# An RWKV attention and channel-mixing kernel: twenty-two transposes taken from TensorE to VectorE and DMA, a new order of the work, hidden values at another address

## The chip, the cores and the metric

The kernel runs on one core of one Trainium2 chip, as one program. The metric is the device time of one execution in microseconds; lower is better. Engines are called as in the profile: PE (TensorE, matrix products; PEld is its weight load), DVE (VectorE), ACT (ScalarE), POOL (GpSimd), SP (the queue that issues all DMAs of this kernel).

## What is computed

Four batches, eight heads, 768 time steps, head dimension 48; then a mixing of the 768 steps with a rank of 32, and a feed-forward part with 384 -> 1536 -> 384 channels. All in float32.

```python
state = 0                                        # per batch and head, 48 x 48
for t in range(768):
    cur = outer(u * k[t], v[t])
    y[t] = r[t] @ (state + cur)
    state = w[t][:, None] * state + outer(k[t], v[t])
x  = y as [batch, 768, 384]
h  = (x.transpose(0, 2, 1) @ U) @ V              # U: 768 x 32, V: 32 x 768
u_ = x + h.transpose(0, 2, 1)
out = u_ + relu(u_ @ w_ch1) @ w_ch2              # 384 x 1536, 1536 x 384
```

## The kernel before, in words

**Tiling.** The 768 steps of a batch are cut into 6 chunks of 128, so there are 24 chunks, numbered 0 to 23 over the batches; heads are handled in four pairs. For each chunk DMAs load the decays (LW), r and k with channels on the partitions (LRK), r and k with time on the partitions (LKR) and v (LV). DVE runs scans of the decays (F, Q), POOL or DVE scale r and k by them (RP, KS). PE then makes the scores inside the chunk (AM), a DVE copy under a mask merges them (CP), and PE forms the chunk's part of y from them (YA) and from the state carried in (YZ). The state is carried on by DS: per head the product of k and v, summed over the 128 steps. For DS, k is needed with time on the partitions, and the scaled k has channels there. So PE turns it (KT: four transposes of 128x128 into PSUM) and ACT or DVE copies the result to SBUF (KN, tile kn).

**x.** The finished y of a chunk is copied to SBUF with channels on the partitions (XE, tile xT). The mixing over time contracts over time, so x is turned as well: XT is three transposes of 128x128 on PE, XN the copy to SBUF (tile xn). Then come the sums with U: for batch 0 a chain GW of six steps, one per chunk, which adds into one PSUM tile; for the other batches GA in two parts (chunks 0 to 3, each in its own quarter of the array's columns, then 4 and 5), a copy G4 and one product SELM that adds the four quarters. The result is split into a high and a low part (GS, GSL), and HP multiplies it by V for each of three channel tiles. u_ is formed and split into high and low parts (UADD, UH, UL).

**Feed-forward.** float32 products are made from three products of a reduced type: high x high, low x high, high x low. For each half batch of 384 steps there are twelve UP steps (one per 128 hidden channels) and twelve DN steps (three channel tiles, four parts each). Every UP and every DN is a group of nine matmuls of 128x384; the text calls it a group. Behind each UP, ACT or DVE write the high part (HH) and DVE the low part (HL) of the hidden values, tiles hh and hl, taken from PSUM tiles of which three exist. They lie in a pool of 24 equal buffers. Small uint8 tiles named gap... shift the addresses of what follows them.

**Order.** Each of these is a step with an engine, the steps it comes after, and the buffers it takes and gives back. A string ORDER of three characters a step (number, and how) fixes the order in which all steps are written, the engine where there is a choice (`alt`), and how many units of idle matmuls (`warm`) PE does first. Each engine runs its instructions strictly in that order. SP is one such queue: a DMA that waits for a buffer holds back every DMA behind it. Weights are loaded as bits and split in the first part of the run (LRAW, AB, E, C1, C2, SG, ADD, HI, SUB).

In lines: KT and KN are `turn_k` (L532) and `copy_k`; XT and XN are in `turn` (L668 and `back`); GA, G4, SELM and GW are in `token_mix` (L691, L697, L701, L720); UP is L824, HL L837, DN L859, the last sum O L874 and its store OUT L878. The address of a buffer follows from the sizes ahead of it in its pool: in this kernel the u tiles start at 201792 (64 modulo 256 bytes) and the first of the hidden buffers at 100032 (192 modulo 256), all others of a pool being whole multiples of 256 bytes further.

Of the kernel before, what the change touches and what calls it, by code (L numbers as in the profile page):

```python
# [8 lines left out]
F32 = mybir.dt.float32  # L9
# [6 lines left out]
AF = mybir.ActivationFunctionType  # L16
# [6 lines left out]
P = 128  # L23
# [16 lines left out]
HALF = P // 2  # L40

# [5 lines left out]
def channel_order():  # L47
# [13 lines left out]
    "3i03j03k03n03v03o13p03q03w+3r13s03x04804B03y14904a03m00704J04D03+O4E03-04d04b01b01104004A03z14K6500090080420"  # L61
    "4e15104L04G04100c04F14QG0K04C14f04M14l14N14m00A04g04i00B05S01204R04400001c00C11J01e04h11401305T00D04c04n04sC"
    "4314q01d03l05301504o01f04r05B14p01610E00H05805501g14O04P04t05600F05CM4500e01715415u05711804V05V08e01910104W0"
    "0I01L05D04S00301h05205E00L04X05X04T05d15a05Y05F05G05I01i01j05H05v04Y00T04x04U14y05x05J04Z00M08U04z04605y15Z1"
    "4700200d04u04v00400f04w10N05z00g05e05f05K05k00O08v06315i05g05U00512900P15h05j05+05W15N00600h15L05M11t06409M0"
    "0G08u08X06505-10i15O06F05P00l06605l04+06001K08V06G05p00J00j00k15m05w06718f14-05Q01u01M00Q00V01v01w09U00R00S0"
    "1N01O16801x05q08g15n05R06906H01A08x01P15r05s05o15t06A48c06B00U08Z01y19006C00n08z08a08b11z06I06J08h06D08W0920"
    "9108i08j06N08y16E08+09K01C08k00W01Q00X08l06K01S08o01+01R16L00Y18-08m06M08n08d09m09L00Z09801B01-06O06P06S06T0"
    "0m01D06U00a12B01E06Q06V06X06Y06Z09A09V08Y16a00b06W08q06f02A02C09301F19416R02D01U0DA01G11k09n02E19509N00o06b0"
    "6c09601H02F02R06g02G00p07709901I19P00q12H06d06h07109Q09W07808w09701T06e06x01m07901V01l00r01W07201n00u01X06y0"  # L70
    "1o06i07301p16z01Y19S10s08p06u01Z08r02j01q19X06j06v01a12009B09a01r00t01s09b06+00v08s09p02k09R12S06k00w02l09F0"
    "0x00y09G0Af09c02U09C00z12m0Ao08t09u12V00+16w07S07T0A009r02T02W19O12I09Y02n09Z00-09s0A102o16r06s16t06-01009D0"
    "2102X17402s09E17507009d02209H02302406l02p02q19t12512612a02Y02r16m02-07606o02J06n02K02L02713Q06p02M02802N12O1"
    "A209h09i09e03807W06q09I02Z17X07a07U07b02b02c02d02P02e07A09j07B02t02f02Q12u07C02g03002v02h02w03102i17D09v03Z0"
    "7G03903202x02y13H0Ae03A03303B07Y09T03403513C02z07V12+13D17E03603J07H07I07c13I03717F03E03F07Z1AC03a03K09w03G0"
    "3L07d17J03M1AF03R03b03N17K03c09J13S03O03P17M07n08309q07o0An09x19f0AE08407N03T0AH08503d03e1AD03f19k07k0AK13U0"
    "3V13W17p07l18003X07m07e03g18109g1Ap19o0Aq0820AG17h09l0Ah0Ar0AM07f13Y0AL0AS0Aj0Ak07L0AT13h07i07O07P09y07g07j0"
    "7q0AN1AI07z07Q0Ai1Am09z07r1D90AO07s0860870DZ07R0DJ09+07w0Al1AJ07+08808908A09-0AP0AQ0A30AU0AR0DK1DL0A40A70AV0"
    "E907-0A508B0A61A80Au0A91AW07x0AZ07y0DC0EA1Db0Aa0AA0DM0DI0DH0Dj0As1At1EB0AX07t07u0AB07v0Av0DN0DE0Di0EC0Ag0DF0"
    "D-0Dc0Da0Dk1De0Df0FT0Ab1DO08C08D08E08F0Dg1AY08G08I0DD0E20E30Dl1Aw0FU1Ax0A-0ER0Ac0Ad1E408J08K0Dh0Ay08L0FV1E00"  # L80
    "E71EU08M0Az08N08O0A+0E50E80B00B10Dd0Ea0DP0DG08P0DB0DQ1Dm0EW0Dp0B20Dq1DT0Eb0ED1ES0DU0B30E61DR0B40EF0EE0B50B90"
    "B60EG08Q0Et0DS0Ec1BA0FW08R0BD0B71BB1F10EH0BC0BE0DV0BF08H0EI0B80Dt0BG18S0EZ0Dr0C70BZ0C80Dn1Bi0Ba18T0E10Bj0DW1"
# [12 lines left out]
    "JR0HL0Jm0Jn1Jr0K50JU0J40HV0JS1K00H40J50JV0Jv0Jw0Jx0H51H60H30KE0Js0JW0JX1Jt0KF0HA0HG0HH0Ju0HW1KG0HB1HC0HI0KH0"
    "Jy0HY0HX0KI0Jz1KJ0HZ0KK1IC0ID0HS0HT1HU0Ha0Hb0Hc0Hd0KL0KM0He0KN0Hf0KO0Hg0KP0KQ0KR0KS0KV0K70Hh0Hi03t0KW0Hk05A0"
    "4j0KZ0Hl0KT0KX0KY1Hm0Ka0KU1Kb1Kc1L80Hj0Ky0L91LA0Hn0Kz0K+04k05b0Kv0Kd0Kw1Ke0Ho0Hp0Kf0Kx0Kj05c0Km0Kn1Ko0Kg0610"
    "Kp0Kk1Kl0Kq1Kh0Ki0L50L60K-0L70LB0Kr0L00L10Ks0L20Kt1Ku0LC0LD0L31L40LE0LH0LF0LT0LX0LY0LU0LV1LZ1LI0LJ0La0Lb0LK0"
    "Lc0LG0Ld16204H0Le0LL0LN0LM0LW1LO03u0Lo0LP0M404I0LQ0Lp1Lq0M50LR0M60LS0Lx0Ly1Lz0L+0Ll0Li0Lm1Ln0Lj0Lf0Lk0L-0M00"
    "Lr0Lg0Lh0Lu0Lv1M70Ls0Lt0MA0Lw0M10MB0M80MC0MD0M21M30ME0M90MF0MG0MJ0MK0ML0MM0MH0MN0MO0MP0MQ0MI0MR0MS0MT0MU0"  # L100
# [53 lines left out]
def rwkv_moe_kernel(ctx, tc, wT, rkT, vN, rkN, uB, uT, uD, U, V, w1, w2, out):  # L154
# [90 lines left out]
    const.tile([P, 96], mybir.dt.uint8, name="gap2")  # L245
    ready = {}

    stage.tile([P, 96], mybir.dt.uint8, tag="gap", name="gap3", bufs=1)

    def split_raw(key):  # L250
# [18 lines left out]
        def absolute():  # L269
# [10 lines left out]

        nm = f"{kind}{i}"
# [3 lines left out]
            "E " + nm, "ACT", lambda: nc.scalar.activation(d["w"], d["low"], AF.Copy, scale=2.0**-29), [l], use=[braw],  # L285
# [81 lines left out]
    sts = {}  # L367

    def chunk(g):
# [164 lines left out]
        def copy_k(eng):  # L534
            st["kn"] = sb2.tile([P, NP, P], F32, tag="kn", name=f"kn_{g}")
            copy(eng, st["kn"], st["trk"])
# [123 lines left out]
    def turn(b, c, after, bx, bxn):  # L660
        blk, cc = divmod(c, TB // P)
        btr = Buf("tr")
        d = {}

        def go():
            tr = d["tr"] = psT.tile([P, NP, P], F32, tag="tr", name=f"trx_{b}_{c}")
            for ct in range(NCT):
                nc.tensor.transpose(tr[:, ct, :], blocks[b, blk][:, ct, cc * P : (cc + 1) * P], ident)  # L668

        def back(eng):  # L670
            xn = d["xn"] = sb2.tile([P, NCT, P], F32, tag="xn", name=f"xn_{b}_{c}", bufs=NCH)
# [10 lines left out]
    def token_mix(b):  # L682
# [3 lines left out]
        def part(cs):  # L686
            if cs[0] == 0:
                d["ga"] = psF.tile([P, DM], F32, tag="ffn", name=f"ga_{b}")
            for c in cs:
                p0 = 32 * (c % 4)  # L690
                nc.tensor.matmul(  # L691
                    d["ga"][p0 : p0 + 32, :], U_sb[:, c, :], xns[b, c]["xn"], start=(c < 4), stop=(c >= NCH - 4)
                )
# [5 lines left out]
        def total():  # L699
            d["gb"] = psF.tile([P, DM], F32, tag="ffn", name=f"gb_{b}")  # L700
            nc.tensor.matmul(d["gb"][0 : 3 * RANK, :], sel, d["g4"], start=True, stop=True)  # L701
# [10 lines left out]
        if b == 0:  # L712
            sums, ga = [], None

            def whole(c):
                if c == 0:
                    d["gb"] = psF.tile([P, DM], F32, tag="ffn", name=f"gb_{b}")
                for i in range(3):
                    to = d["gb"][RANK * i : RANK * (i + 1), :]
                    nc.tensor.matmul(to, U_sb[:, c, :], xns[b, c]["xn"], start=(c == 0), stop=(c == NCH - 1))  # L720

            for c in range(NCH):
                ga = step(
                    f"GW {b}.{c}", "PE", lambda c=c: whole(c), xns[b, c]["steps"] + ready.get(("U", 0), []) + [ga],
                    take=[bgb] if c == 0 else [], use=[bgb, xns[b, c]["buf"]],
# [84 lines left out]
    def ffn(b, blk, dst=None):  # L810
# [37 lines left out]
        for ct in range(NCT):  # L848
# [23 lines left out]
            def total(ct=ct):  # L872
                o = blocks[b, blk][:, ct, :]
                nc.vector.tensor_tensor(out=o, in0=d["o", ct], in1=o, op=ALU.add)  # L874

            def send(ct=ct):
                to = out[b] if dst is None else dst
# [212 lines left out]
```

## Time and profile before

| | |
|---|---|
| device time, three runs | 437.16 us median (437.0 to 438.32) |
| the profiled execution | 437.29 us |
| its span, first to last instruction | 435.6 us |
| granted PE clock, mean | 0.997 of full speed (2.4 GHz) |
| busy: PE, PEld, DVE, ACT, POOL | 426.8, 393.8, 285.1, 167.2, 122.9 us |
| all DMA packets, share of 16 DMA engines | 34.6% |

PE is at work all the time that the page can see; the other engines have room, but not everywhere. The page's busy time of a matmul is from its start to its modelled end, and matmuls overlap, so the length of a group is read from the start of its first matmul to the start of the next group's first.

### The profile page before, as it was taken

To read this page: it belongs to the slowest core of one execution; us is meant where nothing else is said; L and a number is where in the kernel's file an instruction comes from. 1 tells how busy PE (TensorE), PEld (TensorE's weight loads), DVE (VectorE), ACT (ScalarE), POOL (GpSimd) and SP (SyncE) were. 2 spreads that over 40 slices of the span, in tenths; PEclk is the share of its full clock that TensorE was granted. 3 is DMA by queue.
4 is the path that set the end of the run, shared out by engine and by line. 5 is a ranking of instruction groups with operands and counts; after the bars stand their busy time and mean duration, and the time that the engine had idled before them with its cause. 6 is when DMAs were issued, how large, how long until landed. Compare 5 with 4: busy or idle time off the path is not lost. (4 is left out here: it accounts for less than half of the span.)

```text
span 435.6 us, 10589 instructions
## 1 busy us (share of the span) xinstructions
PE 426.8 (98%) x4436; PEld 393.8 (90%) x4436; DVE 285.1 (65%) x584; ACT 167.2 (38%) x421; POOL 122.9 (28%) x131
## 2 busy tenths in 40 slices
PE   8989999999999999999999999999999999999995
PEld 4676688999999899999999999999999899999995
DVE  8899999998989778554986259652445145333501
ACT  3989999896251322023332222231231212100200
POOL 6566858433643130210434221111000000010000
PEclk9999999999999999999999999999999999999998
DMA  7988676652526252321532522111000122020001
GB/s 235 372 281 301 190 240 211 202 182 77 157 67 234 84 162 71 93 88 41 167 103 77 167 86 68 58 50 57 20 25 2 42 50 61 0 62 18 2 2 57
DMA packets 21363, 48.58 MB, mean 112 GB/s; under 512 B 2496, under 2 KB 9024, under 8 KB 21312
## 3 DMA queue, kind: packets, MB, share of 16 engines
q1 hardware_dynamic: 21312, 47.87, 34.0%
q8 instruction: 36, 0.59, 0.6%
q14 instruction: 15, 0.12, 0.1%
HBM read 43.14 MB, written 4.72 MB: 110 GB/s over the span
## 5 line engine op out<-in xcount | busy, mean ns | idle before, releaser
L824 PE MATMUL f<-u,w1h 128*128 128x384 f32 x576 | 148.5, 339 | 1.0 <-DVE hl L837 0.7
L824 PEld LDWEIGHTS f<-u,w1h 128*128 128x128 f32 x576 | 102.7, 188 | 2.9 <-DVE hl L837 1.9
L859 PE MATMUL f<-hh,w2h 128*128 128x384 f32 x288 | 98.4, 342 | 0.0
L859 PE MATMUL f<-hl,w2h 128*128 128x384 f32 x288 | 96.9, 336 | 0.0
L859 PE MATMUL f<-hh,w2l 128*128 128x384 f32 x288 | 96.8, 336 | 0.0
L824 PE MATMUL f<-u,w1l 128*128 128x384 f32 x288 | 96.8, 336 | 0.0
L831 ACT ACTIVATE hh<-f 128x384 fp32r<-128x384 f32 x60 | 28.9, 494 | 110.3 <-PE f L824 110.3
L837 DVE SCALAR_TENSOR_TENSOR hl<-f,hh 128x384 fp32r<-128x384 f32 x96 | 51.4, 552 | 27.6 <-ACT hh L831 26.8
L859 PEld LDWEIGHTS f<-hh,w2h 128*128 128x128 f32 x288 | 54.1, 188 | 1.5 <-issue 1.4
L859 PEld LDWEIGHTS f<-hl,w2h 128*128 128x128 f32 x288 | 54.1, 188 | 0.1
L824 PEld LDWEIGHTS f<-u,w1l 128*128 128x128 f32 x288 | 54.1, 188 | 0.0
L859 PEld LDWEIGHTS f<-hh,w2l 128*128 128x128 f32 x288 | 54.0, 188 | 0.0
L783 POOL TENSOR_TENSOR u<-xT,u 128x384 fp32r<-128x384 f32 x10 | 10.6, 1061 | 104.5 <-DVE u L779 97.0
L833 DVE TENSOR_SCALAR hh<-f 128x384 fp32r<-128x384 f32 x36 | 19.8, 552 | 28.9 <-PE f L824 28.8
L874 DVE TENSOR_TENSOR xT<-f,xT 128x384 f32<-128x384 f32 x24 | 13.2, 550 | 31.6 <-PE f L859 25.8
L552 DVE COPY_PREDICATED A<-masks,aps 128x1024 f32<-128x1024 uint32 x24 | 31.7, 1320 | 3.3 <-ACT A L479 2.3
L416 DVE TENSOR_TENSOR_SCAN F<-w,bank 128x129 f32<-128x129 f32 x96 | 32.4, 399 | 1.5 <-issue 1.0
L481 POOL TENSOR_SCALAR_AFFINE_SELECT A<-dv 128x512 f32<-128x512 f32 x31 | 20.6, 677 | 41.7 <-DVE hl L837 17.6
L430 DVE TENSOR_TENSOR_SCAN Q<-w,bank 128x516 f32<-128x516 f32 x24 | 29.3, 1221 | 1.0 <-PE bank L559 0.7
L436 POOL TENSOR_TENSOR rk<-rk,Q 128x512 f32<-128x512 f32 x17 | 20.9, 1228 | 31.9 <-DVE Q L430 18.9
L479 ACT ACTIVATE A<-ident,dv 128x128 f32<-128x128 f32 x68 | 21.3, 390 | 19.0 <-PE trk L532 11.9
L440 POOL TENSOR_TENSOR rk<-rk,F 128x512 f32<-128x512 f32 x17 | 20.8, 1224 | 27.5 <-DVE F L416 22.0
(123 smaller groups left out, 576.8 us busy)
## 6 DMA issues: line engine op xcount, KB each, us to landing
rk<-in_rkT SPq DMA_DIRECT2D x24, 512.0 KB, 4.5
raw_w<-in_w SPq DMA_DIRECT2D x24, 384.0 KB, 4.7
w<-in_wT SPq DMA_DIRECT2D x30, 258.5 KB, 3.0
kr<-in_rkN SPq DMA_DIRECT2D x18, 384.0 KB, 3.9
v<-in_vN SPq DMA_DIRECT2D x24, 224.0 KB, 3.6
out_dram<-xT SPq DMA_DIRECT2D x24, 192.0 KB, 1.9
raw_V<-in_V SPq DMA_DIRECT2D x1, 192.0 KB, 4.0
raw_U<-in_U SPq DMA_DIRECT2D x1, 192.0 KB, 5.7
```

Of the source, the lines that this page charges most:

```text
L416: nc.vector.tensor_tensor_scan(out=out, data0=st["row"][:, j * SEG + 1 : (j + 1) * SEG + 1][:, ::-1], data1=zeros[:, 0:SEG], initial=1.0, ...
L430: nc.vector.tensor_tensor_scan(out=flat(st["Q"]), data0=flat(st["w"]), data1=zeros, initial=1.0, op0=ALU.mult, op1=ALU.add)
L436: ENG[eng].tensor_tensor(out=rk[:, 0], in0=rk[:, 0], in1=st["Q"][:, :, 0:P], op=ALU.mult)
L440: ENG[eng].tensor_tensor(out=k, in0=k, in1=st["F"], op=ALU.mult)
L479: nc.scalar.activation(A[:, i, j], ident, AF.Copy, scale=dv[:, NP * i + j : NP * i + j + 1])
L481: nc.gpsimd.affine_select(out=A[:, i], in_=dv[:, NP * i : NP * i + NP].unsqueeze(2).broadcast_to([P, NP, P]), pattern=[[0, NP], [1, P]], c ...
L552: nc.vector.copy_predicated(by_j(st["A"]), mask8, by_j(st["aps"]))
L824: nc.tensor.matmul(ps, wt[:, f, ct, :], u[ct][:, z], start=(n == 0), stop=(n == 8))
L831: nc.scalar.activation(hh, d["ps", f], AF.Relu)
L833: nc.vector.tensor_scalar(out=hh, in0=d["ps", f], scalar1=0.0, scalar2=None, op0=ALU.max)
L837: nc.vector.scalar_tensor_tensor(out=hl, in0=d["ps", f], scalar=0.0, in1=hh.bitcast(F32), op0=ALU.max, op1=ALU.subtract)
L859: nc.tensor.matmul(d["o", ct], wt[:, 4 * ct + part, f - 3 * part, :], hid[f][z], start=(part == 0 and n == 0), stop=(part == 3 and n == 8),)
```

## The change

Ten of the key turns (chunks 12 to 16 and 18 to 22) and twelve of the x turns (all chunks of batches 2 and 3) no longer go over PE. In their place DVE transposes 32x32 blocks where they stand (KD: one instruction of 128x512; XD: three of 128x128), SP stores the tile to a DRAM buffer (KW, XW), and four DMAs load it back, each into 32 partitions and with the blocks in their new places, in runs of 32 floats (KB, XB). SP issues the four only when the store has landed. The reader (DS or GA) waits for all four.

```diff
+TURN_K = (12,13,14,15,16,18,19,20,21,22)
+TURN_X = (12,13,14,15,16,17,18,19,20,21,22,23)
...
+    def by_dma(kind, nm, after, buf, tile):
...
+            d["at"] = dram.tile(list(t.shape), F32, tag="turn", name=f"turn_{kind}_{nm}", bufs=4)
+            nc.sync.dma_start(d["at"], t)
...
+            t, at = tile(), d["at"].rearrange("(q a) n (s b) -> s a n q b", q=4, s=4)
+            for s in range(4):
+                to = t[32 * s : 32 * s + 32].rearrange("a n (q b) -> a n q b", q=4)
+                nc.sync.dma_start(to, at[s])
...
+        w = step(f"{kind}W {nm}", "SP", there, [after], use=[buf])
+        return step(f"{kind}B {nm}", "SP", back, [w], use=[buf])
...
+            nc.vector.transpose(out=st["kn"].rearrange("p j t -> p (j t)"), in_=st["rk"][:, 1].rearrange("p j t -> p (j t)"))
...
+            if g in TURN_K:
+                kn = step("KD " + nm, "DVE", blocks_of_k, [ks], take=[buf["kn"]], use=[buf["rk"]])
+                kn = by_dma("K", nm, kn, buf["kn"], lambda: st["kn"])
...
+            for ct in range(NCT):
+                nc.vector.transpose(out=d["xn"][:, ct, :], in_=blocks[b, blk][:, ct, cc * P : (cc + 1) * P])
```

The rest: the second part of GA cuts its two matmuls into halves of 192 columns on all four quarters; batch 0 sums its first four chunks by GA and SELM and only the last two by GW; the copy of a turned key leaves out the unused columns; the last sum and its store come in two halves; two of the gap tiles grow by 128 bytes, so that the hidden buffers start at 100160 (64 modulo 256) and u stays at 64; one step of the weights' splitting (E) may run on POOL and does so twice.

```diff
-    const.tile([P, 96], mybir.dt.uint8, name="gap2")
+    const.tile([P, 224], mybir.dt.uint8, name="gap2")
...
+            for n, c in enumerate(cs):
+                for half in range(4 // len(cs)):
+                    p0 = 32 * (n * 4 // len(cs) + half)
...
+            pieces = 2 if (b, blk, ct) == (B - 1, 1, NCT - 1) else 1
```

And the order of all steps is another one; of its table one line of each stands here.

```diff
-    "3i03j03k03n03v03o13p03q03w+3r13s03x04804B03y14904a03m00704J04D03+O4E03-04d04b01b01104004A03z14K6500090080420"
+    "3i03n03j03p03q03o13v13s13k03r13w+3x03+84804B04D04903y10704a03m04b04A01101b03-04J00804E04004G05004d04KM3z1410"
```

Three places show what it does. The first is PE at the end of batch 3's attention, behind YZ of its last chunk, 23 (y_23 is its output, trx the turned x, f1 and f2 the outputs of UP and DN). Before:

```order
L631 MATMUL y_23_4506<-rk_23_3641,Z_22_4476 32x128 x8
L635 MATMUL y_23_4506<-rk_23_3641,Z_22_4476 32x128 x4
L668 MATMUL trx_3_4_4540<-ident_98,xT_3_1_4409 128x128 x3
L859 MATMUL f2_2_1_0_4544<-hh_2_1_0_4173,w2h_127 128x384
L859 MATMUL f2_2_1_0_4544<-hl_2_1_0_4174,w2h_127 128x384
```

Now:

```order
L666 MATMUL y_23_4516<-rk_23_3984,Z_22_4510 32x128 x8
L670 MATMUL y_23_4516<-rk_23_3984,Z_22_4510 32x128 x4
L874 MATMUL f1_2_1_9_4551<-u_2_1_0_3987,w1h_125 128x384 x2
L874 MATMUL f1_2_1_9_4551<-u_2_1_0_3987,w1l_126 128x384
L874 MATMUL f1_2_1_9_4551<-u_2_1_1_4086,w1h_125 128x384 x2
```

The turn of chunk 22's x (3.4) is gone from there, and no other turn follows; ten groups of UP and DN stand between this place and GA, its reader.

The second place is SP for the same x, from the load of v for chunk 23 on (turn_X are the DRAM buffers, 3.3 to 3.5 the chunks of batch 3's second half). Before:

```order
L878 DMA out_dram<-xT_0_2565 128x384
L398 DMA v_4395<-in_vN 128x448
L878 DMA out_dram<-xT_1_3173 128x384
L386 DMA w_0_4671<-in_wT 128x517
L386 DMA w_2_4685<-in_wT 128x517
L878 DMA out_dram<-xT_1_3173 128x384
```

Now:

```order
L424 DMA v_4419<-in_vN 128x448
L384 DMA turn_X_3.4_4549<-xn_4_4496 128x384
L384 DMA turn_X_3.5_4611<-xn_5_4577 128x384
L390 DMA xn_4_4496<-turn_X_3.4_4549 32x12x32 x4
L384 DMA turn_X_3.3_4623<-xn_3_4573 128x384
L390 DMA xn_3_4573<-turn_X_3.3_4623 32x12x32 x4
L390 DMA xn_5_4577<-turn_X_3.5_4611 32x12x32 x4
L932 DMA out_dram<-xT_1_3216 128x384
```

Three stores and twelve loads stand where there was none, and the loads of 3.3 and 3.5 end last.

The third place is SP for the first key that is turned this way, chunk 12. Before, the load of v for chunk 12 and the loads behind it:

```order
L398 DMA v_2360<-in_vN 128x448
L394 DMA kr_2384<-in_rkN 128x768
L390 DMA rk_2391<-in_rkT 128x1024
L381 DMA w_2437<-in_wT 128x517
L394 DMA kr_2459<-in_rkN 128x768
```

Now:

```order
L424 DMA v_2280<-in_vN 128x448
L384 DMA turn_K_2283<-kn_2191 128x512
L390 DMA kn_2191<-turn_K_2283 32x16x32 x4
L407 DMA w_2311<-in_wT 128x517
L416 DMA rk_2359<-in_rkT 128x1024
```

The loads of the decays of chunk 16 and of r and k of chunk 14 now stand behind a wait for a store. DS 12 stands on PE behind the sums of batch 1 (GA, AM 12, SELM), as it did.

## Rows read from the trace of the kernel before

**Rows 1.** The page, part 1: busy us, share of the span, instructions.
```profile
PE 426.8 (98%) x4436; PEld 393.8 (90%) x4436; DVE 285.1 (65%) x584; ACT 167.2 (38%) x421; POOL 122.9 (28%) x131
```

**Rows 2.** Busy time by stretch, in us, with the number of instructions.
```profile
core 0: us, PE busy (x) PEld busy (x) DVE busy (x) ACT busy (x) POOL busy (x), PEclk, DMA share, GB/s
20.00:40.00 20.00, 18.48 (x385) 14.06 (x385) 19.88 (x46) 18.35 (x51) 13.60 (x14) 1.00 0.89 301
67.20:98.50 31.30, 30.62 (x353) 29.23 (x352) 30.59 (x66) 28.66 (x62) 17.50 (x17) 1.00 0.63 199
147.00:200.00 53.00, 53.00 (x574) 50.07 (x574) 34.38 (x69) 14.64 (x39) 11.37 (x11) 1.00 0.35 108
```

**Rows 3.** Groups by line: out<-in, shapes, count | busy us, mean ns | idle before.
```profile
L668 PE MATMUL trx<-ident,xT 128*128 128x128 f32 x72 | 12.5, 282 | 1.0 <-ACT kn L167 0.6 <-ACT xT L167 0.4
L532 PE MATMUL trk<-ident,rk 128*128 128x128 f32 x80 | 12.5, 278 | 0.0
L720 PE MATMUL gb<-xn,U_sb 128*32 128x384 f32 x36 | 4.8, 490 | 0.0
```

**Rows 4.** Timeline of PE around a key turn: start us, length us, what.
```profile
304.12 0.60 PE L532 MATMUL trk<-ident,rk 128*128 128x128 f32 x4
304.48 0.42 PE L859 MATMUL f<-hh,w2h 128*128 128x384 f32 x1
...
306.14 0.51 PE L824 MATMUL f<-u,w1h 128*128 128x384 f32 x2
```

**Rows 5.** Timeline of PE: an HP behind YZ, and an x turn.
```profile
269.79 0.44 PE L765 MATMUL hp<-Vst,gs 96*128 96x384 f32 x1
270.07 0.51 PE L824 MATMUL f<-u,w1h 128*128 128x384 f32 x2
...
276.31 0.49 PE L668 MATMUL trx<-ident,xT 128*128 128x128 f32 x3
276.56 0.59 PE L824 MATMUL f<-u,w1h 128*128 128x384 f32 x2
...
278.20 0.33 PE L765 MATMUL hp<-Vst,gs 96*128 96x384 f32 x1
```

**Rows 6.** Timeline of PE: first and last of eight UP, then of four DN.
```profile
357.85 0.51 PE L824 MATMUL f<-u,w1h 128*128 128x384 f32 x2
...
370.33 0.34 PE L859 MATMUL f<-hh,w2h 128*128 128x384 f32 x1
...
375.03 0.34 PE L859 MATMUL f<-hh,w2h 128*128 128x384 f32 x1
...
381.32 0.51 PE L765 MATMUL hp<-Vst,gs 96*128 96x384 f32 x2
```

**Rows 7.** Timeline of PE: both parts of GA of batch 2.
```profile
238.54 1.46 PE L691 MATMUL ga<-xn,U_sb 128*32 128x384 f32 x12
239.93 0.44 PE L859 MATMUL f<-hh,w2h 128*128 128x384 f32 x1
```

**Rows 8.** Groups by line on DVE, columns as in rows 3.
```profile
L169 DVE COPY kn<-trk 128x512 f32<-128x512 f32 x4 | 2.7, 682 | 1.7 <-PE trk L532 1.7
L169 DVE COPY xn<-trx 128x384 f32<-128x384 f32 x9 | 5.0, 552 | 4.1 <-PE trx L668 4.0
L779 DVE CAST u<-xT 128x384 fp32r<-128x384 f32 x12 | 4.9, 422 | 0.1
```

**Rows 9.** DMA: issues; then packets of 396.7 to 399.2, of 4.2 to 4.95.
```profile
w<-in_wT SPq DMA_DIRECT2D x30, 258.5 KB, 3.0
out_dram<-xT SPq DMA_DIRECT2D x24, 192.0 KB, 1.9
...
q1 hardware_dynamic: 144, 0.20, 22.0%
...
DMA packets 230, 0.22 MB, mean 293 GB/s; under 512 B 160, under 2 KB 160, under 8 KB 230
q1 hardware_dynamic: 230, 0.22, 90.2%
```

**Rows 10.** SP: who waited for whom, us in total, times, longest; an issue.
```profile
SPq L878 <- DVE xT L874: 159.5, 17, 28.2
...
380.53 0.34 SPq L878 DMA_DIRECT2D out_dram<-xT  x1
```

More of the change, by code (lines that the diff above doesn't have):

```diff
@@ L66 @@
[L66 to L70, printed above, removed]
@@ L284, in split_raw @@
         lo = step(
[L285 removed]
+            "E " + nm, "ACT", rounded, [l], use=[braw], alt="Pool",
         )
@@ L688, in part @@
                 d["ga"] = psF.tile([P, DM], F32, tag="ffn", name=f"ga_{b}")
[L689 to L693, printed above, removed]
+            for n, c in enumerate(cs):
+                for half in range(4 // len(cs)):
+                    p0 = 32 * (n * 4 // len(cs) + half)
+                    cols = slice(half * DM * len(cs) // 4, (half + 1) * DM * len(cs) // 4)
+                    nc.tensor.matmul(
+                        d["ga"][p0 : p0 + 32, cols], U_sb[:, c, :], xns[b, c]["xn"].rearrange("p c t -> p (c t)")[:, cols],
+                        start=(c < 4), stop=len(cs) < 4 or b == 0,
+                    )
         def copy4():
@@ L712, in token_mix @@
         if b == 0:
-            sums, ga = [], None
             def whole(c):
-                if c == 0:
-                    d["gb"] = psF.tile([P, DM], F32, tag="ffn", name=f"gb_{b}")
                 for i in range(3):
                     to = d["gb"][RANK * i : RANK * (i + 1), :]
-                    nc.tensor.matmul(to, U_sb[:, c, :], xns[b, c]["xn"], start=(c == 0), stop=(c == NCH - 1))
-            for c in range(NCH):
+                    nc.tensor.matmul(to, U_sb[:, c, :], xns[b, c]["xn"], start=False, stop=(c == NCH - 1))
+            xn4 = [s for c in range(4) for s in xns[b, c]["steps"]]
+            ga = step(
+                f"GA {b}.0", "PE", lambda: part(range(4)), xn4 + ready.get(("U", 0), []), take=[bga],
+                use=[xns[b, c]["buf"] for c in range(4)],
+            )
+            g4 = step(f"G4 {b}", "ACT", copy4, [ga], take=[bg4], use=[bga])
+            ga = step(f"SELM {b}", "PE", lambda: total(False), [g4], take=[bgb], use=[bg4])
+            for c in range(4, NCH):
                 ga = step(
                     f"GW {b}.{c}", "PE", lambda c=c: whole(c), xns[b, c]["steps"] + ready.get(("U", 0), []) + [ga],
-                    take=[bgb] if c == 0 else [], use=[bgb, xns[b, c]["buf"]],
+                    use=[bgb, xns[b, c]["buf"]],
                 )
@@ L870, in ffn, with total, send @@
                 )
[L872 to L877, printed above, removed]
-                nc.sync.dma_start(to[ct, :, blk * TB : (blk + 1) * TB], blocks[b, blk][:, ct, :])
-            o = step(f"O {b}.{blk}.{ct}", "DVE", total, [prev] + keeps, use=[bps, bx])
-            step(f"OUT {b}.{blk}.{ct}", "SP", send, [o], use=[bx])
+            pieces = 2 if (b, blk, ct) == (B - 1, 1, NCT - 1) else 1
+            for piece in range(pieces):
+                at = slice(piece * TB // pieces, (piece + 1) * TB // pieces)
+                def total(ct=ct, at=at):
+                    o = blocks[b, blk][:, ct, at]
+                    nc.vector.tensor_tensor(out=o, in0=d["o", ct][:, at], in1=o, op=ALU.add)
+                def send(ct=ct, at=at):
+                    to = out[b] if dst is None else dst
+                    nc.sync.dma_start(to[ct, :, blk * TB + at.start : blk * TB + at.stop], blocks[b, blk][:, ct, at])
+                nm = f"{b}.{blk}.{ct}" + (f".{piece}" if pieces > 1 else "")
+                o = step("O " + nm, "DVE", total, [prev] + keeps, use=[bps, bx])
+                step("OUT " + nm, "SP", send, [o], use=[bx])
     def recurrence(xs):
```

109 lines of the change are left out of this document (67 added, 42 removed).

## The prediction, made before the changed kernel ran

> **What bounds the kernel now.** I read the busy times first [rows 1]: TensorE works 426.8 of 435.6 us, no other engine over 65%. Then the stages [rows 2]. In the first 98 us VectorE is as full as TensorE (19.88 of 20 us, 30.59 of 31.30), because scans, masks and the splitting of the weights fall there. From 98 us on TensorE alone is full (53.00 of 53.00 us between 147 and 200, VectorE 34.38). So a microsecond of matrix work that goes after 98 us is a microsecond of the end, and one that goes earlier is mostly not. The time outside the span is 437.29 - 435.6 = 1.7 us; the profiled execution lies 0.13 us over the median, so I start from 437.3.
>
> **What leaves TensorE.** All 22 turns that go (10 of keys, 12 of x) belong to batches 2 and 3, that is to the full stage. The page gives 12.5 us for 80 key and 12.5 for 72 x matmuls [rows 3], but matmuls overlap, so I take start to start. A key turn holds the engine from 304.12 to 304.48, 0.36 us [rows 4]; an x turn from 276.31 to 276.56, 0.25 us [rows 5]. 10 x 0.36 + 12 x 0.25 = 6.6 us.
>
> Each turn also slows what follows: the DN group behind the key turn takes 306.14 - 304.48 = 1.66 us [rows 4], in an undisturbed stretch (381.32 - 375.03) / 4 = 1.57 [rows 6]; the UP group behind the x turn 278.20 - 276.56 = 1.64 [rows 5] against (370.33 - 357.85) / 8 = 1.56 [rows 6]. That is 0.085 us for each of 22, 1.9 us. It doesn't go everywhere: where a turn stood between small matmuls and a big group, the small ones now meet the big group. An HP behind YZ takes 0.28 us [rows 5], an undisturbed large matmul 1.57 / 9 = 0.17, so such a meeting costs 0.1; by the order of both programs there are five more, +0.5. Net 1.4 us.
>
> **GA.** Both parts of a batch take 239.93 - 238.54 = 1.39 us [rows 7], two rounds of 384 columns, about 0.7 each. The second has two chunks and so uses half the array's columns; cut into halves of 192 columns on all four it should take half, 0.35. Three batches: 1.0 us.
>
> **Addresses of the inner values.** In the kernel before, u lies at 64 modulo 256 bytes and the hidden values at 192. A UP group (reads u) takes 1.560 us, a DN group (reads hidden values) 1.573 [rows 6]. If the address is the whole difference, 96 DN groups give 1.2 us; if it is none of it, zero. A loss has no row for it: the u matmuls already run at the new residue. I take 1.1.
>
> **Batch 0's sums.** 36 matmul records of GW, 4.8 us [rows 3], become one GA part (0.7), one SELM (about 0.35) and two GW (a third, 1.6): 2.1 us less. But it lies where VectorE is the full engine [rows 2], and by the two orders VectorE has about as many steps before the first DN as it had (three fewer); the new order also puts 91 instead of 73 units of idle matmuls there. I take 0, and -2 as the bound.
>
> **The end.** The last sum and its store are cut in halves: one more VectorE instruction, half the bytes behind it. Both are tenths of a microsecond; 0.
>
> **What is added, and what covers it.** (1) VectorE turns blocks. No row shows this operation. A copy of 512 elements out of PSUM takes 682 ns, a cast of 384 inside SBUF 422 [rows 8]: a key turn 0.55 to 0.8 us, I take 0.7; an x turn is three of 128 elements, 0.25 each. 10 x 0.7 + 12 x 0.75 = 16 us, less 3 KN (0.68) and 8 XN (0.55) that leave it [rows 8], +9.6 us on an engine that is free for a third of that stage [rows 2]. Cover: three PSUM buffers, so that TensorE is 1.56 us a group away from any hl it needs; without that cover each turn would cost up to its 0.7. The Trainium skill ("VectorE: DVE Perf Modes", The three transpose paths) gives 311 ns for a 128x128 bf16 turn; by it an x turn would be an estimated 0.93 us, and the sum the same; no row here shows it.
>
> (2) The W store: 256 or 192 KB; a 192 KB store lands in 1.9 us, a 258.5 KB load in 3.0 [rows 9]. (3) The B load: four DMAs of 32 partitions, in runs of 128 bytes: 2048 packets for keys, 1536 for x, that is 128 or 96 for each of 16 engines. SP needs 0.34 us for an issue [rows 10], so 1.4 for four. A packet's price has rows on both sides. Above: a 1536-byte store, 144 packets in 22.0% of 16 x 2.5 us, 61 ns with its semaphore packets, about 66 without [rows 9]. Below: in the first stretch of loads 230 packets took 90.2% of 16 x 0.75 us = 10.8 us; at the store's rate (1536 bytes in 66 ns) their 0.22 MB are 9.4 us, which leaves 9 ns for each of 160 packets under 512 bytes [rows 9]. In size 128 bytes lies next to those: 13 ns by a straight line. Then B takes 1.4 us of issue, 1.7 or 1.2 of packets and some 2 to land, and a whole W and B about 7 us.
>
> (4) SP waits for W to land before it issues B, and what stands behind waits too: at KW 12, KB 12 it is LW 16 and LRK 14. SP already stands 159.5 us at OUT alone waiting for VectorE [rows 10] without TensorE losing time, so its queue has room. What counts is the cover of each B until its reader. Counted in the new order by the group times above: KB 12 to DS 12 about 4 us; XB 2.5 to GA 2.1 about 10; XB 3.3 and 3.5, two of three in a row, to GA 3 about 5 from their issue; KB 22 to DS 22 about 9; the others 9 to 55. Only KB 12 is short, by 1 to 2 us: +1.5.
>
> **Sum.** 437.3 - 6.6 - 1.4 - 1.0 - 1.1 + 1.5 = **428.7 us**.
>
> **Rivals.** *Small packets are dear* (slower). If a 128-byte packet costs what a 1536-byte one does, 66 ns, a key B takes 8.4 us and an x B 6.3. DS 12 then waits 8.5 us, GA 2.1 behind KB 18 and XB 2.5 about 7, GA 3 behind three B in a row about 7, DS 19 and DS 22 three together: 25 us against a gain of 10, 437.3 - 10.1 + 25.5 = 453. It turns at some 45 ns a packet. For it: no row here has 128 bytes, and each B writes 32 partitions only. Against: 32-byte packets at 9 ns [rows 9]. The Trainium skill ("DMA: Bandwidth & Descriptors", Specifications) asks for transfers of at least 512 bytes for line rate and says that shorter ones are read, modified and written; that rule speaks for this rival, and the 9 ns of the rows speak against it. Chance 0.13.
>
> *Partly late.* Two or three B wait 1 to 3 us each, through SP's queue (a W that waits for a late VectorE turn holds a load that TensorE needs) or at 25 to 40 ns a packet: +4 to +7 us, 432 to 436. For it: 22 new places where one queue waits. Against: SP's slack [rows 10]. Chance 0.16.
>
> *Nothing changes*: the waits eat the whole gain, 436 to 438.5; it needs just 10 us of them. Chance 0.04.
>
> *More goes.* Batch 0's 2 us count and DS 12 doesn't wait: 437.3 - 12.1 = 425, and down to 423 if the new order loses the few waits of the old. Chance 0.12.
>
> **Numbers.** The forecast, 426 to 432, has 0.55. What a measurement can tell from no change is about 0.3%, 1.3 us. Faster: 0.55 + 0.16 + 0.12 = 0.83; same 0.04; slower 0.13. The range runs over the forecast, the partly late and the case where more goes: 423.5 to 436.5.
>
> **What would show it.** TensorE's busy time about 10 us lower; 40 key matmuls instead of 80, 36 of x instead of 72; DN groups at 1.56 us in the quiet last stage (address) or still at 1.57; the second GA round at 0.35 us; the issue-to-landing of the B DMAs at 3 to 4 us (mine) or over 8 (dear packets); among TensorE's waits, bank behind kn and ga behind xn. I am wrong if ga or bank wait over 5 us for a DMA, or if HL falls behind VectorE's turns.

## The result, and the profile after

The changed kernel took 429.15 us in the median of four runs (428.44 to 429.74), the kernel before 437.15 beside it: a ratio of 0.9818, 95% interval 0.9807 to 0.9829, 8.0 us less. In a second set of runs it took 428.10 us beside 437.41 (0.9793, 0.9769 to 0.9818). Two executions of the experiments below were slow, one of keys_back (1447 us) and one of gw_back (686 us); without them the two medians are 435.59 and 429.33 us. The forecast was 428.7 us, with a range of 423.5 to 436.5.

The profiled execution took 429.74 us with a span of 428.0. The page's busy times, to be read against [rows 1]:

```profile
PE 415.9 (97%) x4363; PEld 386.0 (90%) x4369; DVE 292.8 (68%) x622; ACT 160.6 (38%) x407; POOL 123.1 (29%) x133
```

TensorE works 10.9 us less (forecast: about 10), VectorE 7.7 us more. By stretch, with the columns of [rows 2]:

```profile
20.00:40.00 20.00, 17.80 (x383) 14.45 (x381) 19.78 (x43) 18.01 (x52) 16.01 (x16) 1.00 0.86 280
67.20:98.50 31.30, 29.89 (x334) 28.33 (x333) 29.25 (x69) 27.59 (x59) 9.46 (x10) 1.00 0.68 223
147.00:200.00 53.00, 52.83 (x538) 50.41 (x538) 42.92 (x89) 15.68 (x45) 18.63 (x18) 1.00 0.63 162
```

The picture is the old one: VectorE full early, TensorE full from about 98 us on. In the late stretch VectorE went from 34.38 to 42.92 us and the DMA engines from 0.35 to 0.63, and TensorE is still full. The groups that answer [rows 3] and [rows 8] (line, engine, operation, tiles, shapes, count | busy, mean ns of one | idle before):

```profile
L703 PE MATMUL trx<-ident,xT 128*128 128x128 f32 x36 | 6.2, 282 | 0.4 <-ACT dv L536 0.4
L558 PE MATMUL trk<-ident,rk 128*128 128x128 f32 x40 | 6.3, 281 | 0.2 <-issue 0.2
L737 PE MATMUL ga<-xn,U_sb 128*32 128x192 f32 x24 | 1.5, 326 | 0.0
...
L712 DVE STREAM_TRANSPOSE xn<-xT 128x128 f32<-128x128 f32 x36 | 8.2, 280 | 0.0
L567 DVE STREAM_TRANSPOSE kn<-rk 128x512 f32<-128x512 f32 x10 | 6.9, 695 | 1.2 <-issue 1.1
```

40 key and 36 x matmuls are left, as forecast. A key turn takes VectorE 0.695 us (forecast 0.7), an x turn 3 x 0.28 (forecast 3 x 0.25). The Trainium skill ("VectorE: DVE Perf Modes", The three transpose paths) gives 311 ns for a 128x128 turn of two-byte values; the trace's 280 ns for four-byte values lies a little below it.

The DMA side, to be read against [rows 9]: packets of the whole execution, the queue's share, and the way of the turned keys (issues, KB each, median us to landing):

```profile
DMA packets 64996, 58.55 MB, mean 137 GB/s; under 512 B 43184, under 2 KB 51376, under 8 KB 64944
...
q1 hardware_dynamic: 64944, 57.83, 46.3%
...
turn_K<-kn SPq DMA_DIRECT2D x10, 256.0 KB, 3.3
kn<-turn_K SPq DMA_DIRECT2D x40, 64.0 KB, 2.8
```

38,912 packets of 128 bytes are new; one took 13.2 ns in the mean of the trace (forecast 13, bounds 9 and 66). Behind the first DN groups TensorE's waits, in all, are this row (engine, tile, line <- what it waited for: us in total, times, longest):

```profile
PE f L874 <- DVE hl L887: 0.2, 1, 0.2
```

No wait for a turned block anywhere, so also none at DS 12, where the forecast had put 1.5 us. What SyncE itself waited for (us in total, times, longest), with [rows 10] before it, how it issued the first turned block's four loads, and their reader, DS 12, on TensorE:

```profile
SPq L932 <- DVE xT L928: 60.9, 13, 13.2
...
SPq L390 <- DMA turn_K<-kn: 8.2, 5, 2.8
...
140.29 2.71 SPq L390 DMA_DIRECT2D kn<-turn_K  x4
...
147.13 0.56 PE L590 MATMUL bank<-v,kn 128*48 128x48 f32 x16
```

Its 159.5 us behind OUT shrank to 60.9, and four loads take 2.71 us to issue, not the 1.4 of the forecast. That number becomes important below.

**Where the time went.** For a finer account I took TensorE's matmuls in order and summed, for each kind of step, the time from its start to the start of the next one. I call *late part* what runs from the group DN 0.0.0.2 to the end of TensorE's last matmul; in the kernel before the same work begins two DN groups (3.12 us) behind its first DN at 84.46. Its length is 343.4 us before and 333.43 after, and in two later executions of the same late order, after_again and end_whole, it is 333.45 and 333.44.

| late part, us | before | after | difference | forecast |
|---|---|---|---|---|
| key turns | 4.31 | 0.41 | -3.90 | -3.6 |
| x turns | 4.67 | 1.27 | -3.40 | -3.0 |
| GA | 4.33 | 3.32 | -1.01 | -1.0 |
| DN groups | 150.02 | 148.36 | -1.66 | -1.1 address, and drag |
| UP groups | 133.34 | 132.81 | -0.53 | drag (-1.9 with DN) |
| scores, sums, mixes | 46.79 | 47.28 | +0.49 | +0.5 |
| sum | | | -10.0 | -10.1, and +1.5 at DS 12 |

The rest is outside it: the part before ended at 87.58 us before (84.46 + 3.12) and at 89.17 in this execution of after, but at 87.45 in another; and from TensorE's last matmul to the end of the span it is 4.54 us before and 5.42 after.

### The profile page after: what moved, and what is told of

It is laid out like the page before. It is cut to its first block, busy times and chain, and to the rows that moved or that the text cites. A ratio compares the mean times of both kernels' runs of the same rounds, so it can differ in the third digit from the quotient of the medians.

```text
span 428.0 us, 10667 instructions
## 1 busy us (share of the span) xinstructions
PE 415.9 (97%) x4363; PEld 386.0 (90%) x4369; DVE 292.8 (68%) x622; ACT 160.6 (38%) x407; POOL 123.1 (29%) x133
## 5 line engine op out<-in xcount | busy, mean ns | idle before, releaser
L881 ACT ACTIVATE hh<-f 128x384 fp32r<-128x384 f32 x51 | 25.3, 498 | 118.9 <-PE f L874 118.8
L883 DVE TENSOR_SCALAR hh<-f 128x384 fp32r<-128x384 f32 x45 | 24.7, 552 | 31.9 <-PE f L874 31.7
L833 POOL TENSOR_TENSOR u<-xT,u 128x384 fp32r<-128x384 f32 x13 | 13.4, 1046 | 98.4 <-ACT u L827 95.0
L928 DVE TENSOR_TENSOR xT<-f,xT 128x384 f32<-128x384 f32 (+1 forms) x25 | 13.3, 534 | 33.0 <-PE f L909 27.3
L507 POOL TENSOR_SCALAR_AFFINE_SELECT A<-dv 128x512 f32<-128x512 f32 x30 | 19.4, 662 | 47.7 <-PE y L653 25.9
L462 POOL TENSOR_TENSOR rk<-rk,Q 128x512 f32<-128x512 f32 x14 | 18.1, 1291 | 25.4 <-DVE Q L456 14.0
L491 POOL TENSOR_TENSOR kr<-kr,u_rep 128x384 f32<-128x384 f32 x16 | 16.4, 1030 | 29.9 <-DVE kr L488 29.6
L505 ACT ACTIVATE A<-ident,dv 128x128 f32<-128x128 f32 x72 | 22.8, 388 | 5.0 <-PE f L874 3.2
```

The lines of the kernel that those rows point to most:

```text
L462: ENG[eng].tensor_tensor(out=rk[:, 0], in0=rk[:, 0], in1=st["Q"][:, :, 0:P], op=ALU.mult)
L491: ENG[eng].tensor_tensor(out=st["kr"][:, 0], in0=st["kr"][:, 0], in1=u_rep, op=ALU.mult)
L505: nc.scalar.activation(A[:, i, j], ident, AF.Copy, scale=dv[:, NP * i + j : NP * i + j + 1])
L507: nc.gpsimd.affine_select(out=A[:, i], in_=dv[:, NP * i : NP * i + NP].unsqueeze(2).broadcast_to([P, NP, P]), pattern=[[0, NP], [1, P]], c ...
L881: nc.scalar.activation(hh, d["ps", f], AF.Relu)
L883: nc.vector.tensor_scalar(out=hh, in0=d["ps", f], scalar1=0.0, scalar2=None, op0=ALU.max)
```

## The experiments

Times are medians; "late part" is that of the account above, which tells smaller differences than the run times do. The kernel before took 437.39, 437.53 and 437.41 us beside the three sets.

### Turns back on TensorE: turns_back, keys_back

```diff
-TURN_K = (12,13,14,15,16,18,19,20,21,22)
-TURN_X = (12,13,14,15,16,17,18,19,20,21,22,23)
+TURN_K = ()
+TURN_X = ()
```
keys_back empties TURN_K alone. In ORDER, KT and KN (XT and XN) stand where KB (XB) stood.

> The kernel after with all 22 turns of batches 2 and 3 back on TensorE, each with its copy out of PSUM on ScalarE, put where the load of the turned blocks stood; everything else, order included, is that of after. Theory (the turns' own start-to-start time and the drag on the group behind): 10 x (0.36 + 0.085) + 12 x (0.25 + 0.085) = 8.5 us less some meetings of small and large matmuls that move back, so 436.5 to 437.7 us, TensorE busy about 10 us more than the 415.9 of after. Rival (the gain came with the new order, the turns were covered anyway): under 4 us more, 430 to 433. Rival (a turn on TensorE costs only its 0.36 and 0.25, no drag): 6.6 more, 435.8.

> The kernel after with only the 10 key turns back on TensorE. Theory: 10 x (0.36 + 0.085) = 4.4 us more than after, about 433.6. Rival (no drag): 3.6 more, 432.8. Rival (order alone): within 1 us of after. What turns_back has over this is the price of the 12 x turns: 4.0 us by the theory, 3.0 without drag.

turns_back: 440.97 us (ratio to before 1.0073, 1.0050 to 1.0096); late part 346.4, 13.0 us more than after. keys_back: 435.63 us; late part 340.5, 7.1 more, where the theory said 4.4. So the turns carry the gain: with all of them put back by hand, the new order, the addresses and the halves of GA together are 3.6 us slower than the kernel before. But 13.0 is 4.5 us more than my theory's 8.5. TensorE's busy time in turns_back is the 426.8 us of [rows 1] again:

```profile
PE 426.8 (97%) x4445; PEld 393.4 (89%) x4445; DVE 281.2 (64%) x576; ACT 169.9 (39%) x429; POOL 122.8 (28%) x133
```

and its waits in the late part are new:

```profile
PE gb L747 <- ACT A L504: 0.9, 1, 0.9
PE trk L557 <- issue: 0.7, 1, 0.7
PE trx L702 <- ACT kn L169: 0.6, 1, 0.6
PE trx L702 <- ACT xn L169: 0.6, 1, 0.6
PE f L873 <- DVE xT L927: 0.5, 1, 0.5
```

3.3 us of the 13.0 are waits, two of them for the copy that must free the one PSUM buffer of the turns, where I had put two turns close together. What makes up the other 1.2 us over the theory stays open. The kernel before had its turns placed so that its late part had no such wait. What a turn costs therefore depends on the order around it: by the account above the 22 turns and their drag were worth 7.9 us where they stood, and put back by hand they cost 13.0.

### The addresses: addr_back

```diff
-    const.tile([P, 224], mybir.dt.uint8, name="gap2")
+    const.tile([P, 96], mybir.dt.uint8, name="gap2")
...
-    stage.tile([P, 224], mybir.dt.uint8, tag="gap", name="gap3", bufs=1)
+    stage.tile([P, 96], mybir.dt.uint8, tag="gap", name="gap3", bufs=1)
```

> The kernel after with the two gaps of 224 bytes back at 96, so that the inner values lie at 192 modulo 256 bytes again and u stays at 64; nothing else. Theory (the address is the whole difference between a UP and a DN group): a DN group of 9 matmuls takes 1.573 instead of 1.560 us, 96 groups give +1.2 us, about 430.4. Rival (the address is nothing, the order of the operands is): 0, 429.15, and DN groups stay at 1.560.

429.42 us: by the run times not to be told from after (429.15, 428.10). The trace tells it. Six DN groups in a row on TensorE, first and last matmul and what follows, in after and then in addr_back:

```profile
284.57 0.34 PE L909 MATMUL f<-hh,w2h 128*128 128x384 f32 x1
...
293.93 0.34 PE L874 MATMUL f<-u,w1h 128*128 128x384 f32 x1
```
```profile
283.27 0.34 PE L909 MATMUL f<-hh,w2h 128*128 128x384 f32 x1
...
292.70 0.51 PE L874 MATMUL f<-u,w1h 128*128 128x384 f32 x2
```

9.36 / 6 = 1.560 us a group in after, 9.43 / 6 = 1.572 in addr_back; the late part is 334.5, 1.1 us longer. Summed by kind, the DN groups take all of that, and every other kind is the same to 0.1 us, though other tiles that lie between the two gaps moved as well. So the address of the hidden values is the difference between UP and DN groups, and the term of 1.1 was right. Two places stay unexplained: the first nine DN groups of the kernel before (84.46 to 98.50) already ran at 14.04 / 9 = 1.560 at the old address, and so did six of addr_back, between 229 and 239 us.

### GA's second part: ga_whole

```diff
-            for n, c in enumerate(cs):
-                for half in range(4 // len(cs)):
-                    p0 = 32 * (n * 4 // len(cs) + half)
...
+            for n, c in enumerate(cs):
+                p0 = 32 * n
+                nc.tensor.matmul(d["ga"][p0 : p0 + 32, :], U_sb[:, c, :], ...)
```

> The kernel after with the second part of GA in batches 1 to 3 as two matmuls of 384 columns a chunk instead of four of 192 over all column groups; nothing else. Theory (trace of after: GA takes 1.108 instead of 1.39 us a batch): +0.28 x 3 = +0.85 us, about 430.0, GA at 1.39. Rival (the array is busy elsewhere for the same time, halves bring nothing to the end): 0.

429.23 us; late part 334.6, 1.2 more than after. Both parts of GA on TensorE, in after (first fence) and in ga_whole:

```profile
144.38 1.18 PE L737 MATMUL ga<-xn,U_sb 128*32 128x384 f32 x16
145.49 0.45 PE L579 MATMUL aps<-rk 48*64 48x128 f32 x8
```
```profile
142.94 1.48 PE L735 MATMUL ga<-xn,U_sb 128*32 128x384 f32 x12
144.36 0.45 PE L579 MATMUL aps<-rk 48*64 48x128 f32 x8
```

1.11 against 1.42 us a batch, 0.9 us in three, and 0.2 in what follows. The second round takes about 0.4 (1.11 less half of 1.42), where the forecast said 0.35.

### The first 98 us: gw_back, early_before

```diff
-            xn4 = [s for c in range(4) for s in xns[b, c]["steps"]]
-            ga = step(f"GA {b}.0", "PE", lambda: part(range(4)), ...)
-            g4 = step(f"G4 {b}", "ACT", copy4, ...)
-            ga = step(f"SELM {b}", "PE", lambda: total(False), ...)
-            for c in range(4, NCH):
+            ga = None
+            for c in range(NCH):
```
early_before has this too, and runs the steps that the kernel before has ahead of its first DN in that kernel's order (LRK 12 apart), the others in the order of after.

> The kernel after with batch 0 summed by six GW steps of three matmuls a chunk again, in place of the four-column GA part, its copy, SELM and two GW; the first four at GA's place in after's order, and the five units of idle matmuls ahead of SELM gone with it. Theory (VectorE bounds the first 98 us): within 0.5 us of after. Rival (TensorE bounds there after all): +2 us, about 431. Third (the chain of GA, copy and SELM is what made the early part later): 0.5 to 1 us less.

> The kernel after with the kernel before's order (and its six GW sums of batch 0) up to the first DN group, and after's order from there; the turns by VectorE and DMA, the addresses and the GA halves stay. Theory (by the traces the same work ends 1.6 us later in after: HP 0.1.2 ends at 89.17 with two DN groups of 1.56 done, in before at 84.46): 1.6 us less than after, about 427.5. Rival (VectorE is full there in both orders, what isn't done early is done later): 0, 429.15. Rival (the seam of the two orders makes TensorE wait for VectorE): up to 2 us more, 431.

gw_back: 429.38 us, late part 333.5: the late part is that of after, though ahead of it four GW (2.7 us together) stand on TensorE in place of a GA part of 0.8 and a SELM of 0.6. What they cost ahead of it the run doesn't decide. Its late part begins at 89.05 us. In the eleven traces of kernels whose order up to there is that of after it begins nine times between 87.36 and 88.10, once at 86.31 (more_turns) and once at 89.17 (the first of after); the kernel before stands at 87.58. One trace at the upper end of that scatter, and a time 0.2 us over the 429.15 of after and 1.3 over its 428.10, leave anything from 0 to 1.6 us for the four GW.

early_before: 429.11 us. Its late part begins at 88.14, no earlier than most traces of after's order, and my theory that the new order had made the early part 1.6 us later fell: it rested on one execution, the odd one at 89.17. The equal time hides two shifts: the late part is 334.7, 1.2 us longer than in after, because three DN groups at the seam of the two orders (91 to 98 us) take 1.9 to 2.0 us each, and the end behind it is 0.9 us shorter (below).

### How much room the way through HBM has: runs_64, b_split

```diff
                 to = t[32 * s : 32 * s + 32].rearrange("a n (q b) -> a n q b", q=4)
-                nc.sync.dma_start(to, at[s])
+                for z in (slice(0, 16), slice(16, 32)):
+                    nc.sync.dma_start(to[..., z], at[s][..., z])
```
That is runs_64 (each run of 128 bytes in two); b_split has `to[z], at[s][z]`, halves of the partitions.

> The kernel after with every load of turned blocks cut into two, each with 64 bytes in a run in place of 128: twice the DMAs on SyncE (0.57 to 0.69 us each) and twice the packets. What it measures is the cover: a turn's way through HBM gets about 2.5 us of issue longer. Theory (each turn has several us of cover; the shortest, KB 12, has about 4): within 0.5 us of after, with packets of 64 bytes at 7 to 13 ns. Rival (cover is nearly used up): two to ten us more, with waits of DS or GA for a DMA in the trace.

> The kernel after with every load of turned blocks cut into two of 16 partitions: as many packets of 128 bytes as in after (38912), but 176 DMAs in place of 88. It tells apart what made runs_64 38 us slower. If the number of packets (38912 more at 10.6 ns, 26 us for each DMA engine) did it: equal to after within 1 us. If the time on SyncE's queue did it (in runs_64 the loads took 114.7 us of issue against 55.5): slower by a good part of 38 us, in the measure in which their issue time grows; should a DMA of half the packets take half the time to issue, SyncE's time is as in after and nothing is lost, and then the issue time goes with the packets.

runs_64 took 467.18 us (1.067, 1.0638 to 1.0703) and b_split 462.15 (1.055, 1.0523 to 1.0576): 38 and 34 us more than after (429.15 and, beside b_split, 428.10). My theory, that every turn has several microseconds of cover, fell, and b_split says what is short. It has exactly the packets of after, at 12.7 ns each, and twice the DMAs. Its first turned block:

```profile
138.89 5.26 SPq L391 DMA_DIRECT2D kn<-turn_K  x8
```

5.26 us for eight; over the whole run each takes 0.63 in the mean, as in after with twice the runs (medians 0.607 and 0.623): what SyncE pays goes with the number of these DMAs, not with their packets. In all 111.1 us of issue instead of 55.5. runs_64 lies 4.9 us higher still, each beside its own set of the kernel before; it has 38,912 packets more, at 10.6 ns, and also 114.7 us of issue, and no run parts the two. TensorE's longest late waits in b_split, and its busy time by stretch (columns of [rows 2]), with the same two stretches of after behind it:

```profile
PE ga L738 <- DMA xn<-turn_X_2.5_3507: 7.8, 1, 7.8
PE y L644 <- DVE xT L172: 7.6, 1, 7.6
PE ga L738 <- DMA out_dram<-xT: 4.9, 1, 4.9
PE y L644 <- DMA v<-in_vN: 2.9, 1, 2.9
```
```profile
200.00:260.00 60.00, 48.61 (x536) 45.66 (x535) 33.56 (x70) 10.22 (x32) 7.48 (x8) 0.92 0.49 131
260.00:380.00 120.00, 107.58 (x1037) 101.57 (x1037) 56.06 (x115) 23.07 (x58) 15.45 (x18) 0.94 0.32 81
...
200.00:260.00 60.00, 60.00 (x666) 56.95 (x666) 41.56 (x86) 15.18 (x45) 13.79 (x15) 1.00 0.61 160
260.00:380.00 120.00, 120.00 (x1089) 116.24 (x1088) 61.66 (x126) 22.21 (x54) 11.14 (x13) 1.00 0.27 69
```

In both stretches TensorE of after works all the time. Here it waits at GA for turned x. The third row is such a wait too, though it names a store: SyncE issues the loads of 3.3 and 3.5 until 362.53 us, and GA of batch 3 starts at 364.79. It also waits for a load (v) and for an x block that have nothing to do with the turns but stand behind them in SyncE's queue: the copy xT of the second row starts at 334.77, when the block's store, issued at 332.52 behind eight loads of turned x (from 327.26 on), is through. That it is this store which frees the block is read from the order, not from a row. In all, the late part is 34.4 us longer, and its waits sum to 26.7. Inside each of the three longest waits the granted clock fell to its lower level (1.2 GHz), for 10.2, 6.8 and 6.8 us; that makes the 0.92 and 0.94 in the mean. SyncE issues DMAs in 144 of the 240 us between 140 and 380 (92 in after); in much of the rest it waits in order, the W for VectorE (33.6 us) and the B for their W (16.2), and what follows waits too.

The Trainium skill ("DMA: Bandwidth & Descriptors", Issuing engines are not separate DMA queues) says that the time to start a DMA is usually small beside the DMA itself; measured against the packets it is the other way here, 0.63 us of issue against 512 x 13.2 ns / 16 = 0.42 us on each DMA engine; from issue to landing such a load takes 2.8 us in the median.

### Four more turns: more_turns

```diff
-TURN_K = (12,13,14,15,16,18,19,20,21,22)
-TURN_X = (12,13,14,15,16,17,18,19,20,21,22,23)
+TURN_K = (10,12,13,14,15,16,18,19,20,21,22)
+TURN_X = (8,9,10,12,13,14,15,16,17,18,19,20,21,22,23)
```

> The kernel after with four more turns off TensorE: the keys of chunk 10 and x of chunks 2, 3 and 4 of batch 1 (all behind 98 us), with their steps put into VectorE's and SyncE's queues by hand. Theory: 0.36 + 3 x 0.25 + 4 x 0.085 = 1.45 us less, about 427.7, unless the keys of chunk 10 land behind the state's DS 10 at 123.7 (their last load is issued at about 122): then a wait of up to 1 us takes most of it back. Rival (VectorE, over 85% busy there, passes its 3.2 us on to TensorE): no gain or up to 1 us more.

431.54 us, 2.4 more than the 429.15 of after and 3.4 more than its 428.10; late part 336.4, 3.0 more. The trace is of an execution of 430.0 us; the median lies 1.5 higher, and no trace shows where. The waits name the place (TensorE, late part):

```profile
PE bank L590 <- DMA kn<-turn_K: 1.8, 1, 1.8
PE bank L590 <- DVE Z L626: 1.3, 1, 1.3
```

The first is DS 12. The four loads of KB 12 were issued from 142.65 to 145.27 and DS 12 started at 147.27; in after_again (below) they were issued from 138.35 to 141.12 and DS 12 ran at 145.41 without a wait. The loads of x of batch 1, put ahead of them, had pushed them back by 4.3 us, and that was more than the cover. So the short cover that the forecast named is real; it was just not used up. The second is DS 10: here TensorE came earlier (the late part of this execution begins at 86.31, that of after_again at 87.45), but the Z it needs starts on VectorE at 121.81 us, and at 122.02 in after_again, at the end of a chain that begins in both with a load of w (F at 117.89 and 118.11). There this chain sets the time and not TensorE, and a turn less on TensorE only makes it wait. This wait took back the early start; TensorE's last matmul ends 1.9 us later than in after_again, about what DS 12 waited.

### The end: after_again, end_whole, whole_x2

```diff
-            pieces = 2 if (b, blk, ct) == (B - 1, 1, NCT - 1) else 1
+            pieces = 1
```
whole_x2 has that, and TURN_X begins with 8 and 9.

> The kernel after, unchanged, beside the three below on one chip. From the first profiles: the stretch from DN 0.0.0.2 to TensorE's last matmul is 333.4 us in every execution of this order without a wait; the stretch before it ended at 87.4, 87.7 and 89.2 us in three kernels that are the same up to there, so it should end anywhere from 87 to 89.5 here, and the time be 427.5 to 430.

> The kernel after with the last sum and its store whole again. Prediction's reading (tenths either way): 0. New theory from the traces: between TensorE's last matmul and the end of the span lie 4.54 us before and 5.42 after, because eight packets of the second half store stand behind an instruction fetch of 8192 bytes (0.62 us) in one DMA engine; a whole store is issued later and finds the fetch elsewhere, so 4.5 us again and 0.8 us less than after, about 428.3.

> end_whole, and also x of chunks 2 and 3 of batch 1 turned by VectorE and DMA; no key turn more, and nothing put ahead of the loads of the keys of chunk 12, on which more_turns lost 3 us (TensorE waited for the loads of turned keys at DS 10 and DS 12). Theory: 0.8 + 2 x (0.25 + 0.085) = 1.5 us less than after, about 427.6. Rival (the two turns' eight loads, 0.63 us each on SyncE, make DS 12's loads late again): equal to after or slower.

after_again: 428.10 us (428.01 to 429.60), late part 333.4, begun at 87.45; from TensorE's last matmul to the end 5.48. end_whole: 427.29 (426.94 to 427.74), and there 4.69. whole_x2: 426.66 us (426.49 to 427.55; 0.9758 of before, 0.9736 to 0.9780), the fastest of all and 1.4 us under after_again, where the theory said 1.5; its late part is 332.9, the end 4.48 behind it. The last sum and store in the kernel before, in after and in end_whole (VectorE and SyncE):

```profile
431.13 0.56 DVE L874 TENSOR_TENSOR xT<-f,xT 128x384 f32<-128x384 f32 x1 [5.80 <-PEq L1018]
431.72 0.33 SPq L878 DMA_DIRECT2D out_dram<-xT  x1
```
```profile
422.71 0.62 DVE L928 TENSOR_TENSOR xT<-f,xT 128x192 f32<-128x192 f32 x2 [5.68 <-PEq L1073]
423.09 0.81 SPq L932 DMA_DIRECT2D out_dram<-xT  x2
```
```profile
421.03 0.56 DVE L928 TENSOR_TENSOR xT<-f,xT 128x384 f32<-128x384 f32 x1 [5.68 <-PEq L1073]
421.61 0.33 SPq L932 DMA_DIRECT2D out_dram<-xT  x1
```

From the start of the sum to the end of the span (435.57, 428.02, 425.6) that is 4.4, 5.3 and 4.6 us. The halves save 0.2 us until the first store is issued, but the second is out only 1.2 us behind the start of the sum, a whole one 0.9. In the trace of after 248 of the 256 packets of both halves begin by 424.80 us; the other eight, one DMA engine's share of a half, follow from 425.22 to 425.66, directly behind an instruction fetch of 8192 bytes that begins at 424.60 and takes 0.62 us. In the kernel before the fetch comes when the store is through. That the fetch is the cause rests on this order of the packets. Eleven traces have the halves: in ten the last eight packets begin where a fetch ends, and the span ends 5.25 to 5.61 us behind the last matmul; in the eleventh, early_before, the fetch begins before the packets do, and the end comes after 4.57 us.

## Why the prediction was right

The sum was 437.3 - 6.6 - 1.4 - 1.0 - 1.1 + 1.5 = 428.7. Point by point:

- **What bounds it: right.** In the late part every matmul that goes is time that goes: 10.0 us, with 0.2 us of waits in it. The start of the late part did not move beyond its scatter (87.58 before, 87.45 in after_again); whether batch 0's fewer sums were worth the 0 that I took is not shown (gw_back).
- **The turns, -6.6, and drag net -1.4: right in the sum, the sizes shifted.** Start to start they held TensorE for 7.3 us; I had taken the shortest turns of the rows (0.36 and 0.25) where the means are 0.39 and 0.28. The drag on groups was 1.1 us (0.5 on UP, 0.5 on DN besides the address), not 1.9; the small matmuls +0.5 as taken (0.24 on HP, 0.22 on the products for y; that these are the five meetings which I counted is not shown). Net 7.9 against 8.0.
- **GA, -1.0: right** (1.01).
- **Addresses, -1.1: right** (1.1 in addr_back, 1.560 against 1.572 us a group).
- **The end, 0: wrong by 0.9 us.** "Half the bytes behind it" looked at bytes; what ends the program is the last landing, and that came later.
- **DS 12, +1.5: wrong**, it was 0. I had counted 4 us from the loads' issue to DS 12 against 5 that they need; there were 6.8 (140.29 to 147.13), and the loads needed about 4.9 (the last issued at 142.37, and the 2.8 of the profile to land). more_turns shows the wait once they go out 4.3 us later. These last two errors nearly cancelled each other, which is luck: 437.3 - 10.0 + 0.9 is 428.2 where the sum said 428.7 and the two sets measured 429.15 and 428.10.
- **VectorE, +9.6 us: about right** (+7.7), and covered as said; no group of the late part waited longer than 0.2 us for an hl.
- **The price of a packet, 13 ns: right** (13.2), and with it the rival of dear packets fell. The Trainium skill ("DMA: Bandwidth & Descriptors", Specifications) wants transfers of 512 bytes or more for line rate; the trace agrees on the rate (128 bytes in 13.2 ns, 1536 in about 67), but at this volume it cost no time.
- **SyncE's issue, 0.34 us a DMA: wrong**, 0.63. It cost nothing here, but the argument "SP's queue has room" was worth much less than I thought: the rival called partly late had its mechanism right, and b_split, with the issue time doubled, pays 34 us for it. Between no wait at all and that lies only a factor of two.

## What to carry to other kernels

Moving a turn from a full TensorE to an idle VectorE plus a trip through HBM pays its full start-to-start time, as long as the loads come back early enough; count the trip in DMAs on the issuing queue (0.63 us for each of these loads, with 192 to 512 packets in it) before counting packets, and test the cover by doubling the loads. Sum up a change over a fixed stretch of the trace, kind by kind: differences of 1 us that the run times hid stand out there, where equal orders agree to 0.02. And put back what a change adds at the very end of a program on its own: there the last landing counts, not the bytes.

## What the runs showed of the hardware that I had not expected

- A load of blocks (32 partitions, rows of 128 bytes) takes SyncE 0.63 us to issue: 0.62 in the median with 384 or 512 runs of 128 or of 64 bytes, 0.61 with half as many; stores and loads of whole tiles take 0.33 to 0.40 in the median. Packets of 64, 128, 768 and 1536 bytes took 10.6, 13.2, 37 and 67 ns.
- Moving the start of the hidden values from 192 to 64 modulo 256 bytes makes a matmul of 384 columns 1.3 ns shorter (12 ns for nine), nearly everywhere; why nine DN groups of the kernel before and six of addr_back were short at 192 stays open.
- In ten of eleven traces with the halves an instruction fetch of 8 KB stood ahead of one DMA engine's share of the last store (0.62 us in after), and the span ended 5.25 to 5.61 us behind the last matmul; in the eleventh and with a whole store it was 4.48 to 4.69.
- With one and the same order the first 87 us vary by up to 2.9 us between executions (late part begun at 86.31 to 89.17), while the 333 us behind them repeat to 0.02 (after, after_again, end_whole).
